# Weights issued at the turn, two more pairs transposed on TensorE, and one scores chunk moved up in a fused attention and MLP kernel

## The chip, the cores and the metric

One core of a Trainium2 chip. The metric is device time in microseconds of a whole execution. The kernel before has a median of 423.64 us (3 runs, 423.2 to 425.69). A trace's span is 1.7 to 1.8 us shorter than the time of the same run.

## The reference

```
scores = q k^T / 8 ; attn = softmax(scores) ; x = attn v      # 8 batches, 12 heads, 448 tokens, 64 wide
h = x[3584,768] @ w_in[768,2048] ; out = leaky_relu(h, 0.01) @ w_out[2048,768]
```

## The kernel before

Two heads of one batch are a "pair"; there are 48. Pairs 0 to 5 run alone (`first`); then each batch's MLP runs on TensorE with the attention of later pairs cut in between it as "clusters". All loads up to pair 17 (but k and v of pair 0) and all weights go through GpSimd's queue, which casts float32 to bfloat16 on the way; SP issues the later loads, the DMA transposes and the stores. q and k have to be transposed before the scores matmul: on TensorE (into PSUM, with a copy back by VectorE) below `NPE`, by a DMA transpose from `NPE` on; `NXP` does the same for x. A pair's scores come in four "chunks" of 112 keys, and w_out is loaded in four "pieces".

```
    NXP = 9
    NPE = 12
    def dma_transposes(u):
        if NPE <= u < NU:
            turn(qkT[u % NQ][:, :QL], qk_sb[u].rearrange("p i so h d -> p (i so h d)"))
    # ... transposes(u): eight nc.tensor.transpose and one nc.vector.tensor_copy, for u < NPE

    def first(u):
        # ... scores and expo of chunks 0 and 1
        if u >= 1:
            pv(u - 1, 0)
        transposes(u + 1)
        # ... casts and loads
        if u > 0:
            scores(u, 2)
        scores(u, 3)

    def cluster(g):
        # ... transposes(turn_q) if turn_q < NPE, scores, expo, pv, x_transposes
        if r < 3:
            cast(u + 3 + r)
            load(u + 5 + r)
            load_w({9: 1, 10: 1, 13: 1}.get(g, 0))
        if r > 0:
            dma_transposes(u + 2 + r)

    # the turn between the pairs of `first` and the clusters
    transposes(HP + 1)
    cast(HP + 3)
```

The first batch's second matmul takes output columns 0 to 383 for all its rows first, then columns 384 to 767. The last w_out piece (rows 1024 to 2047 of those last columns) is therefore wanted latest.

The softmax here doesn't subtract the row's maximum and nothing guards it: scores larger than these inputs give would overflow.

Of the kernel before, what the change touches and what calls it, by code (L numbers as in the profile page):

```python
# [16 lines left out]
def kernel(  # L17
# [101 lines left out]
    def load(u):  # L119
        if u >= NU:  # L120
            return
        if u < NSW:
            if u % 2 == 0:
                load_soft(u, 2, (0, 1, 2))
            return
        for x in range(3):
            load_one(u, x, nc.sync)

    def cast(u, parts=(0, 1, 2), by=nc.gpsimd.tensor_copy):
        if u >= NU:  # L130
            return
        for x in parts:
            f = raw[u].pop(x)
            if u not in qk_sb:
                qk_sb[u] = cast_pool.tile([SC, 2, NSC, 2, D], BF16, name="qkb")
            if x < 2:
                by(qk_sb[u][:, x].rearrange("p so h d -> p h so d"), f)  # L137
            else:
                by(v_sb[u % NV][:, :, :, :D], f)  # L139
# [8 lines left out]
    def load_w(n=1):  # L148
        for _ in range(n):
            if w_steps:  # L150
                o, i = w_steps.pop(0)
                nc.gpsimd.dma_start(out=o, in_=i)
# [21 lines left out]
    def warm_up(n):  # L174
        for _ in range(n):
            ps = ps_g.tile([P, 512], F32, name="mm", tag="g")
            nc.tensor.matmul(ps, warm[:, :P], warm, start=True, stop=True)
# [15 lines left out]
    x_t = {}  # L193

    NXP = 9
    NPE = 12

    def turn(dst, src):
        nc.sync.dma_start_transpose(out=dst.rearrange("p (c s) -> p c s", s=SC), in_=src)
# [4 lines that stand above are left out]
# [6 lines left out]
    def turn_tile(bank):  # L210
        if bank is None:
            return ps_g.tile([P, 2, S], BF16, name="tr", tag="g")
        return bank.bitcast(BF16)[:, :2 * S].rearrange("p (i s) -> p i s", i=2)

    def transposes(u, bank=None):
        if u >= min(NPE, NU):
            return
        for parts in ((1,), (0,)) if u == 0 else ((0, 1),):
            tr = turn_tile(bank)
            for i in parts:  # L220
                for so in range(NSC):
                    nc.tensor.transpose(  # L222
                        tr[:, i, ts(so, SC)], qk_sb[u][:, i, so], ident[:SC, :SC]
                    )
            at = slice(parts[0], parts[-1] + 1)
            nc.vector.tensor_copy(  # L226
                qkT[u % NQ][:, :QL].rearrange("p (i s) -> p i s", i=2)[:, at], tr[:, at]
            )
# [3 lines left out]
    def scores(u, c):  # L232
        ps = ps_s.tile([P, 2, 512], F32, name="sc", tag="sc")
        t = qkT[u % NQ]
        sc_t[u, c] = ps
        for j in range(2):
            nc.tensor.matmul(  # L237
                ps[:, j, :S],
                t[j * D:(j + 1) * D, S + c * SC:S + c * SC + P],
                t[j * D:(j + 1) * D, :S],  # L240
                start=True, stop=True,
            )

    def expo(u, c):
        e = e_sb[u % NE][:, :EL].rearrange("p (j c s) -> p j c s", j=2, c=NSC)
        nc.scalar.activation(e[:, :, c, :], sc_t.pop((u, c))[:SC, :, :S], AX.Exp, scale=scale)  # L246

    def pv(u, j, bank=None):

        e, vt = e_sb[u % NE], v_sb[u % NV]  # L250
        if bank is None:
            ps = ps_g.tile([P, NSC, D + 1], F32, name="pv", tag="g")
        else:
            ps = bank[:, :NSC * (D + 1)].rearrange("p (q d) -> p q d", q=NSC)
        for qc in range(NSC):
            for c in range(NSC):
                at = (j * NSC + c) * S + qc * SC
                nc.tensor.matmul(  # L258
                    ps[:, qc, :], e[:, at:at + P], vt[:, j, c, :],
                    start=(c == 0), stop=(c == NSC - 1),  # L260
                )
        if j == 0:
            x_t[u] = x_pool.tile([SC, NSC, 2, D], BF16, name="x")
        rec = r_pool.tile([SC, NSC, 1], F32, name="rec")
        nc.vector.reciprocal(rec, ps[:SC, :, D:])  # L265
        nc.vector.tensor_mul(  # L266
            x_t[u][:, :, j, :], ps[:SC, :, :D], rec.to_broadcast([SC, NSC, D])
        )

    def x_transposes(u, bank=None):  # L270
        b, hp = divmod(u, HP)
        at = b * S % NX
        dst = xT[:, hp, at:at + S]
        if u >= NXP:
            turn(dst, x_t.pop(u).rearrange("p so h d -> p (so h d)"))
            return
        tr = turn_tile(bank)
        for so in range(NSC):
            nc.tensor.transpose(tr[:, 0, ts(so, SC)], x_t[u][:, so], ident[:SC, :SC])  # L279
        nc.vector.tensor_copy(dst, tr[:, 0, :])  # L280
# [72 lines left out]
    def supply(u):  # L353

        for what, n in {0: [('qk', 2), ('v', 1), ('v', 2), ('load', 6)], 1: [('qk', 3), ('qk', 4), ('v', 3), ('w', 1)], 2: [('qk', 5), ('v', 4), ('v', 5), ('load', 8)], 3: [('qk', 6), ('v', 6), ('w', 1)], 4: [('qk', 7), ('v', 7), ('w', 1)], 5: [('qk', 8), ('v', 8), ('load', 10), ('w', 1)]}[u]:
            if what == "qk":
                cast(n, (0, 1), fast if n in (2, 3) else nc.gpsimd.tensor_copy)
            elif what == "v":
                cast(n, (2,))
            elif what == "load":  # L360
                load(n)
            else:
                load_w(n)

    def first(u):

        scores(u, 0)
        scores(u, 1)
        expo(u, 0)
        if u == 0:  # L370
            warm_up(2)
        expo(u, 1)
        if u == 0:
            scores(u, 2)
        if u >= 2:
            x_transposes(u - 2)
        if u >= 1:
            pv(u - 1, 0)
        transposes(u + 1)
        if u + 1 < HP:  # L380
            supply(u)
        if u > 0:
            scores(u, 2)
        scores(u, 3)
        expo(u, 2)
        expo(u, 3)
        if u + 1 == HP:
            supply(u)
        if u >= 1:
            pv(u - 1, 1)  # L390


    def cluster(g):
        t, r = divmod(g, 4)
        u = 3 * t
        chunks = [divmod(4 * u + 3 * r + x, NSC) for x in range(3)]
        chunks = [(a, c) for a, c in chunks if a < NU]
        heads = [[(u - 1, 0)], [(u - 1, 1)], [(u, 0), (u, 1)], [(u + 1, 0), (u + 1, 1)]][r]
        heads = [(a, j) for a, j in heads if HP <= a < NU]
        turn_q = {3: u + 3, 0: u + 1, 1: u + 2}.get(r, NU)  # L400
        turn_x = {0: u - 2, 2: u - 1, 3: u}.get(r, 0)
        if turn_q < NPE:
            transposes(turn_q)
        elif len(heads) > 1:
            pv(*heads.pop(0))
        for a, c in chunks:
            scores(a, c)
        for a, c in chunks[:2]:
            expo(a, c)
        late.extend(chunks[2:])  # L410
        if HP <= turn_x < NXP:
            x_transposes(turn_x)
        for a, j in heads:
            pv(a, j)
            if j == 1 and a >= NXP:
                x_transposes(a)
        if r < 3:
            cast(u + 3 + r)
            load(u + 5 + r)
            load_w({9: 1, 10: 1, 13: 1}.get(g, 0))  # L420
        if r > 0:
            dma_transposes(u + 2 + r)

# [2 lines left out]
    for u in range(HP):  # L426
        first(u)
# [14 lines left out]
    expo(HP, 2)  # L442
    x_transposes(HP - 1)
    transposes(HP + 1)
    cast(HP + 3)


# [4 lines left out]
    for i in range(B):  # L452
        work = list(range(begin[i], begin[i + 1])) if i + 1 < B else []
        n = cuts[i + 1] - cuts[i]
        total = MD * KD * n + n // P * MD * DM
        used, done, groups = 0, 0, 0

        def catch_up():
            nonlocal done
            while done < len(work) and (  # L460
                groups >= early[done] if i == 0 else used * len(work) >= total * (done + 1)
            ):
                settle()
                cluster(work[done])
                done += 1

        catch_up()
        for step in mlp(i):
            used += step
            groups += 1  # L470
            catch_up()
# [30 lines left out]
```

## Time and profile before

| what | where | value |
|---|---|---|
| median time | runs | 423.64 us |
| span of the traced run (it took 424.84) | page | 423.1 us |
| TensorE busy | page | 408.6 us, 97% |
| longest wait of TensorE | its waits | 4.6 us, once, for a piece of w_out |
| granted clock after that wait | windows | 0.50 for 5 us |

The prediction shows the lines and reads them.

### The profile page before, as it was taken

To read this page: it belongs to the slowest core of one execution; us is meant where nothing else is said; L and a number is where in the kernel's file an instruction comes from. 1 tells how busy PE (TensorE), PEld (TensorE's weight loads), DVE (VectorE), ACT (ScalarE), POOL (GpSimd) and SP (SyncE) were. 2 spreads that over 40 slices of the span, in tenths; PEclk is the share of its full clock that TensorE was granted. 3 is DMA by queue.
4 is the path that set the end of the run, shared out by engine and by line. 5 is a ranking of instruction groups with operands and counts; after the bars stand their busy time and mean duration, and the time that the engine had idled before them with its cause. 6 is when DMAs were issued, how large, how long until landed. Compare 5 with 4: busy or idle time off the path is not lost.

```text
span 423.1 us, 8937 instructions
## 1 busy us (share of the span) xinstructions
PE 408.6 (97%) x3726; PEld 235.1 (56%) x3726; DVE 103.2 (24%) x292; ACT 228.9 (54%) x324; POOL 105.0 (25%) x177
## 2 busy tenths in 40 slices
PE   7999996999999999999999999999999999999995
PEld 3566663454556656554565656654465666654563
DVE  3652431120132212221132212321032311320021
ACT  5888872266724684467634486456752577214300
POOL 7775744320311211131131213131120200000000
PEclk9899999799999999999999999999999999999999
DMA  8999999884475957779465785769275420230022
GB/s 130 192 201 203 173 174 155 159 222 99 107 159 156 209 109 183 188 138 196 98 156 143 198 147 134 193 134 239 57 170 147 118 56 14 60 85 2 0 76 75
DMA packets 98121, 57.69 MB, mean 136 GB/s; under 512 B 55072, under 2 KB 94496, under 8 KB 98080
## 3 DMA queue, kind: packets, MB, share of 16 engines
q1 hardware_dynamic: 78448, 44.63, 46.7%
q0 software_dynamic: 19392, 12.26, 20.8%
q8 instruction: 29, 0.48, 0.5%
q10 hardware_dynamic: 240, 0.23, 0.2%
q14 instruction: 12, 0.10, 0.1%
HBM read 45.61 MB, written 11.01 MB: 134 GB/s over the span
## 4 chain that ended last, share of the span: by engine, by line
PE 87%; DMA 8%; POOL 2%; DVE 1%; issue 1%; POOLq 0%
PE mm L343 33%; PE mm L314 32%; PE pv L258 12%; PE sc L237 9%; DMA w_out_sb<-in_moe_w_out_dram 4%; DMA fv<-in_v_dram 2%; DMA fk<-in_k_dram 2%; PE tr L222 1%; POOL fq L102 1%; PE tr L279 1%; PE sc L314 1%; DVE x L266 1%; POOL fk L102 0%; POOL v L139 0%; DVE o L347 0%
## 5 line engine op out<-in xcount | busy, mean ns | idle before, releaser
L246 ACT ACTIVATE e<-sc 112x896 bf16<-112x896 f32 x192 | 164.8, 915 | 107.3 <-PE sc L237 107.0
L343 PE MATMUL mm<-w_out_sb,h 128*128 128x384 bf16 x896 | 151.7, 328 | 4.8 <-DMA w_out_sb<-in_moe_w_out_dram 4.6
L314 PE MATMUL mm<-xT,w_in_sb 128*128 128x512 bf16 (+1 forms) x756 | 148.6, 353 | 0.2 <-DVE x L266 0.2
L343 PEld LDWEIGHTS <-h 128*128 128x128 bf16 x896 | 86.3, 98 | 60.6 <-issue 6.3
L314 PEld LDWEIGHTS <-w_in_sb 128*128 128x128 bf16 x768 | 72.9, 98 | 66.2 <-issue 1.2
L329 ACT ACTIVATE h<-mm 128x512 bf16<-128x512 f32 (+1 forms) x126 | 68.7, 545 | 58.7 <-PE mm L314 58.6
L258 PEld LDWEIGHTS <-e 112*128 112x128 bf16 x1536 | 57.3, 98 | 26.7 <-issue 16.2
L139 POOL CAST v<-fv 112x512 bf16<-112x512 f32 x30 | 18.5, 616 | 196.6 <-PE pv L258 184.7
L258 PE MATMUL pv<-v,e 112*128 112x65 bf16 x1536 | 66.1, 195 | 0.2 <-ACT e L246 0.2
L347 DVE COPY o<-mm 128x384 f32<-128x384 f32 x56 | 31.2, 558 | 139.5 <-PE mm L343 139.5
L265 DVE RECIPROCAL rec<-pv 112x4 f32<-112x4 f32 x96 | 17.5, 182 | 152.5 <-PE pv L258 151.8
L237 PE MATMUL sc<-qkT 64*128 64x448 bf16 x384 | 50.2, 361 | 0.9 <-DVE qkT L226 0.9
L266 DVE TENSOR_TENSOR x<-pv,rec 112x256 bf16<-112x256 f32 x96 | 40.7, 424 | 3.5 <-DVE rec L265 0.2
L237 PEld LDWEIGHTS <-qkT 64*128 64x128 bf16 x384 | 13.8, 95 | 18.9 <-issue 10.5
L137 POOL CAST qkb<-fk 112x512 bf16<-112x512 f32 x30 | 18.4, 613 | 0.1
L137 POOL CAST qkb<-fq 112x512 bf16<-112x512 f32 x30 | 18.4, 613 | 0.1
L139 POOL COPY v<-fv 112x512 bf16<-112x512 bf16 x17 | 10.4, 620 | 17.6 <-DMA fv<-in_v_dram 9.0
L137 POOL COPY qkb<-fq 112x512 bf16<-112x512 bf16 x14 | 8.7, 620 | 13.1 <-DMA fq<-in_q_dram 13.1
L226 DVE COPY qkT<-tr 128x896 bf16<-128x896 bf16 (+1 forms) x13 | 7.6, 585 | 8.6 <-PE tr L222 8.5
L137 POOL COPY qkb<-fk 112x512 bf16<-112x512 bf16 x14 | 8.7, 618 | 2.7 <-DMA fk<-in_k_dram 2.7
L222 PE MATMUL tr<-ident,qkb 112*128 112x112 bf16 x96 | 7.6, 219 | 1.3 <-DVE qkb L137 1.3
L222 PEld LDWEIGHTS <-qkb 112*128 112x128 bf16 x96 | 6.0, 100 | 3.3 <-DVE qkb L137 1.8
(30 smaller groups left out, 51.9 us busy)
## 6 DMA issues: line engine op xcount, KB each, us to landing
fk<-in_k_dram SPq DMA_DIRECT2D x31, 224.0 KB, 3.4
fq<-in_q_dram SPq DMA_DIRECT2D x30, 224.0 KB, 3.3
fv<-in_v_dram SPq DMA_DIRECT2D x30, 224.0 KB, 3.8
w_in_sb<-in_moe_w_in_dram POOLq DMA_DIRECT2D x4, 768.0 KB, 11.4
w_out_sb<-in_moe_w_out_dram POOLq DMA_DIRECT2D x4, 768.0 KB, 13.5
out_dram<-o SPq DMA_DIRECT2D x8, 336.0 KB, 2.9
out_dram<-o SPq DMA_DIRECT2D x8, 288.0 KB, 2.6
out_dram<-o SPq DMA_DIRECT2D x8, 240.0 KB, 3.4
```

Source lines behind the costliest of these rows:

```text
L137: by(qk_sb[u][:, x].rearrange("p so h d -> p h so d"), f)
L139: by(v_sb[u % NV][:, :, :, :D], f)
L222: nc.tensor.transpose(tr[:, i, ts(so, SC)], qk_sb[u][:, i, so], ident[:SC, :SC])
L237: nc.tensor.matmul(ps[:, j, :S], t[j * D:(j + 1) * D, S + c * SC:S + c * SC + P], t[j * D:(j + 1) * D, :S], start=True, stop=True,)
L246: nc.scalar.activation(e[:, :, c, :], sc_t.pop((u, c))[:SC, :, :S], AX.Exp, scale=scale)
L258: nc.tensor.matmul(ps[:, qc, :], e[:, at:at + P], vt[:, j, c, :], start=(c == 0), stop=(c == NSC - 1),)
L265: nc.vector.reciprocal(rec, ps[:SC, :, D:])
L266: nc.vector.tensor_mul(x_t[u][:, :, j, :], ps[:SC, :, :D], rec.to_broadcast([SC, NSC, D]))
L314: nc.tensor.matmul(open_t[m][:, :n], w_in_sb[:, kk, ts(m, P)], xT[:, kk, at:at + n], start=(fresh and kk == kks[0]), stop=(kk == KD - 1),)
L329: nc.scalar.activation(h[:, m, :n], open_t.pop(m)[:, :n], AX.Prelu, alpha=0.01)
L343: nc.tensor.matmul(ps[:, :NW], h[:, m, ts(c, P)], w_out_sb[:, m, ts(w, NW)], start=(m == 0), stop=(m == MD - 1),)
L347: nc.vector.tensor_copy(o[c][:, ts(w, NW)], ps[:, :NW])
```

## The change

The intent: have the last weights there in time, take two transposes off the DMA engines while those are loaded with weights and inputs, and give ScalarE its next scores before TensorE stops for the casts of pair 2. The title it came with also names a new spacing of one-transfer pairs and q of the first pair on SP; its diff, complete here, has neither.

```
-    NPE = 12
+    NPE = 14
@@ first(u)
         if u >= 1:
             pv(u - 1, 0)
+        if 0 < u < 2:
+            scores(u, 2)
         transposes(u + 1)
         if u + 1 < HP:
             supply(u)
-        if u > 0:
+        if u >= 2:
             scores(u, 2)
@@ cluster(g)
-            load_w({9: 1, 10: 1, 13: 1}.get(g, 0))
+            load_w({9: 1, 10: 1}.get(g, 0))
@@ the turn
     transposes(HP + 1)
+    load_w()
     cast(HP + 3)
```

More of the change, by code (lines that the diff above doesn't have):

```diff
@@ L195 @@
     NXP = 9
-    NPE = 12
+    NPE = 14
     def turn(dst, src):
@@ L378, in first @@
             pv(u - 1, 0)
+        if 0 < u < 2:
+            scores(u, 2)
         transposes(u + 1)
@@ L381, in first @@
             supply(u)
-        if u > 0:
+        if u >= 2:
             scores(u, 2)
@@ L419, in cluster @@
             load(u + 5 + r)
-            load_w({9: 1, 10: 1, 13: 1}.get(g, 0))
+            load_w({9: 1, 10: 1}.get(g, 0))
         if r > 0:
@@ L444 @@
     transposes(HP + 1)
+    load_w()
     cast(HP + 3)
```

## The prediction

> **What bounds the kernel now.** I read the page's busy shares first, then what TensorE waited for, then the chain that ended last in order of time, then windows around the one hole it shows, then the timelines of the engines that issue the transfers concerned.
>
> ```profile
> PE 408.6 (97%) x3726; PEld 235.1 (56%) x3726; DVE 103.2 (24%) x292; ACT 228.9 (54%) x324; POOL 105.0 (25%) x177
> ...
> PEclk9899999799999999999999999999999999999999
> ```
>
> TensorE is busy 408.6 of 423.1 us; no other engine is over 56%. So work put on TensorE costs its full length, and a gain can come only from TensorE's 14.5 us of idle time or from its clock. The clock row has two dips: slice 2 and slice 8 (a slice is 10.6 us, so slice 8 is 74 to 85 us).
>
> ```profile
> PE mm L343 <- DMA w_out_sb<-in_moe_w_out_dram: 4.6, 1, 4.6
> PE tr L222 <- DVE qkb L137: 1.3, 2, 0.7
> ```
>
> The waits of TensorE hold one large entry: a single 4.6 us for a piece of w_out. The second, 1.3 us in two waits, is for the cast of q and k ahead of TensorE transposes. About 4.6 us before the first data-fed work and 4.2 us of final store (418.8 to 423) are the rest; the change touches neither.
>
> ```profile
> 57.45 17.51 DMA w_out_sb<-in_moe_w_out_dram
> 75.00 2.72 PE mm L343 x8
> 77.72 1.24 PE sc L237 x6
> 78.95 0.99 PE pv L258 x16
> 79.94 5.29 PE mm L343 x32
> 85.74 0.67 PE sc L237 x6
> 86.42 0.62 PE pv L258 x16
> ```
>
> This is the chain. The last w_out piece is issued at 57.45 and lands at 75.0. The work after it is slow: six scores matmuls take 1.24 where the next six take 0.67, sixteen PV matmuls 0.99 against 0.62. The windows say why:
>
> ```profile
> 66.00:70.40 4.40, 4.40 (x40) 2.71 (x38) 1.16 (x3) 2.17 (x3) 0.61 (x1) 1.00 1.59 143
> 70.40:75.00 4.60, 0.03 (x2) 0.00 (x0) 0.00 (x0) 0.00 (x0) 4.13 (x7) 0.80 1.31 139
> 75.00:76.50 1.50, 1.50 (x5) 0.71 (x5) 0.00 (x0) 0.00 (x0) 0.24 (x1) 0.50 1.45 197
> ```
>
> Columns: stretch, then busy time of PE, PEld, DVE, ACT, POOL, granted clock, DMA share, GB/s. TensorE is idle from 70.4 to 75, and comes back at clock 0.50; the windows keep it near 0.5 until 80 and show 1.00 after. From 80 us to the last matmul TensorE has no wait worth a row.
>
> **What the Trainium skill says.** (1) "TensorE: Matmul & The Clock Gate", section "What's actually happening": after about one idle window (some 3.4 us) the array runs at half clock, and some 3.4 us of sustained work free it. The trace agrees: 4.57 us idle, then 0.50 for about 5 us. (2) "DMA: Bandwidth & Descriptors", section "Issuing engines are not separate DMA queues": transfers of SP, ACT and GpSimd share the same 16 DMA engines. The trace agrees: a transpose of q and k on SP, median 4.0 us to landing, took 11.2 and 12.3 when issued at 50.39 and 58.15 among the loads. (3) Same page, "Two DMAs through the same engine are not ordered": descriptors start in order within a queue. Landings on GpSimd's queue around 45 to 75 do come in order of issue (below). (4) "TensorE: Matmul & The Clock Gate", "Part 4: PE-mode transpose": it needs a VectorE copy out of PSUM afterwards; the trace has that copy, 0.62 us.
>
> **The change part by part.** The title also names spacing of the software queue and q of the first pair on SP; the diff holds no such edit, so I price only the diff.
>
> *Weights earlier.* GpSimd issues in program order:
>
> ```profile
> 34.71 0.90 POOL L152 DMA_DIRECT2D w_out_sb<-in_moe_w_out_dram  x1
> 45.77 0.90 POOL L152 DMA_DIRECT2D w_out_sb<-in_moe_w_out_dram  x1
> 48.32 0.88 POOL L152 DMA_DIRECT2D w_out_sb<-in_moe_w_out_dram  x1
> 57.45 0.89 POOL L152 DMA_DIRECT2D w_out_sb<-in_moe_w_out_dram  x1
> ```
>
> The new call sits in the turn between the first pairs and the clusters, just ahead of the cast of pair 9, which ran at 35.6. So the second piece goes out at about 35.6 instead of 45.8, the third at 45.8 instead of 48.3, the fourth at about 49 instead of 57.45: each takes its predecessor's place.
>
> When do they land? Issue plus time to landing, from the DMA view window by window: first piece 46.9; q, k, v of pairs 12/13 48.1, 49.7, 52.7; second piece 57.0; third 63.1; q, k, v of 14/15 65.0, 66.8, 70.8; fourth 75.0. That is one saturated queue. A load of 2 pairs reads 0.46 MB (2 pairs x 2 heads x 448 x 64 x 4 B), a piece 1.57 MB (768 x 2048 x 4 B / 4), so 7.46 MB land in 28.1 us, 265 GB/s. At that rate (estimate) the three loads of a group take 5.2 us. The new order is piece 1, piece 2, 12/13, piece 3, piece 4, 14/15. The total is the same, so the last piece is done at 75.0 - 5.2 = 69.8 at the latest; two transposes leave the DMA engines (next part), which should bring it to 66 to 69. TensorE wants it at 70.4 or, with the added transposes, 71.5. So I expect the wait gone: **-4.57 us**.
>
> With the hole goes the clock dip. Excess over the same work at full clock: matmuls 2.72 - 8 x 5.20/32 = 1.42, scores 1.24 - 0.67 = 0.57, PV 0.99 - 0.62 = 0.37, the next 32 matmuls 5.29 - 5.20 = 0.09. Sum **-2.45 us**.
>
> *TensorE transposes for pairs 12 and 13.* Removes two DMA transposes on SP (50.39 and 58.15); adds 16 transposes and two VectorE copies of 0.62. In the chain eight transposes occupy TensorE 0.53, so **+1.06 us** on the bound engine. The copies lie beside: VectorE is 24% busy, and the scores of pair 12 come one cluster later. PSUM rotation is a bit tighter (two PV back to back after a transpose); the cluster at 41.6 us has this pattern already and costs 0.18. I add **+0.2**.
>
> *Scores of chunk 2 ahead of the transposes, pair 1.*
>
> ```profile
> 11.82 0.55 PE L222 MATMUL tr<-ident,qkb 112*128 112x112 bf16 x4 [0.71 <-DVE qkb L137]
> ...
> 12.90 3.59 ACT L246 ACTIVATE e<-sc 112x896 bf16<-112x896 f32 x4 [1.01 <-PE sc L237]
> ```
>
> (First line from TensorE's timeline, second from ScalarE's.) TensorE is in order: it waits 0.71 for k of pair 2, and the scores behind it starve ScalarE for 1.01. Issued before the transposes they fill that hole. ScalarE then works nearly without a break until 28.3, so it paces this stage; up to 1.0 us could come forward, less what TensorE at half clock (12 to 15 us) and the loads hold back. I take **-0.7 us**.
>
> *Sum:* -4.57 - 2.45 + 1.06 + 0.2 - 0.7 = -6.46; 423.64 - 6.46 = **417.2 us**, a gain of 1.5%.
>
> **Rivals.**
>
> (A) *A new wait takes the old one's place: pair 14.* Its loads now stand behind two pieces and are issued after the delayed pair 12 casts, near 57.5 instead of 53.35. Its k should land near 70 to 71.5 (before: 66.8), the cast takes 0.6, then SP transposes; that took 8.1 us to landing in the crowd at 67.49, 4.0 as the median. So 75.5 to 80. Pair 14 is first read as the third chunk of the cluster that ran at 85.67: new time about 80 (85.67 - 7.02 + 1.06, plus two scores at 0.45). A near thing: against it, 0 to 4 us of slack; for it, a queue less emptied than I think. It would give back 1 to 3 us, and over 3.4 us the clock dip too: 419 to 422. One in seven.
>
> (B) *Pair 12 late for TensorE.* Its load now lands behind the second piece: q and k near 54 to 56 instead of 48.1 and 49.7. TensorE's transposes of it start at about 58. Slack some 1 to 2 us; a miss costs about 1 us.
>
> (C) *The piece is still late.* 69.8 without any relief against a need at 71.5, and issue is early enough, so at most a fraction of a us.
>
> (D) *The weights' wait was hidden anyway.* No: TensorE's 0.03 us busy in 4.60, and a chain that runs through that transfer, speak against it.
>
> (E) *More than I count:* relief from the DMA transposes and the early start could also save the first clock dip (about 1.5 us at 12 to 15). That gives 416.
>
> **Range and chances.** The clock and the wait together are 7.0 us and should go as one; the additions are firm. Best plausible 423.64 - 7.0 - 1.5 - 0.5 + 1.2 = about 415.8; A or B in part gives about 420.2. For over 2% the time has to fall under 415.2, which needs every item at its best: 5%. Slower by over 2% means over 432, a new stall far beyond the one removed: 2%.
>
> **What would show it.** Right: no w_out row in TensorE's waits over 0.5 us; clock near 1.00 from 70 to 80; 112 transposes for q and k on TensorE (now 96) and 34 on SP (now 36); the last w_out issue near 49 and landed before 70; ScalarE's idle before its second run of exponentials near 0 instead of 1.01; the end of the span earlier by the same 6 to 7 us that the start of the 96-matmul run (376.71 in the chain) is. Wrong: a row of TensorE waiting for the transposed q and k of pair 14 near 78 to 82, or for the cast of pair 12 near 58, with a clock dip behind it; or an idle GpSimd queue, which would mean that the saturation I count on isn't there.

## The result, and the profile after

418.73 us (median of 4 runs, 418.22 to 419.01) against 424.25 (4 runs) in the same rounds: ratio 0.9866, interval 0.9832 to 0.99. A ratio here is the mean time of one kernel's runs over that of the other's of the same rounds, so it is not quite the ratio of the medians. Two later sets of rounds with the same pair gave 0.9903 and 0.9897. So the change is faster, by 1.0 to 1.3%, which is within 2%; the time is inside the range of 415.8 to 420.2 and 1.5 us over the point of 417.2.

The page after, busy shares and clock:

```profile
PE 407.5 (98%) x3742; PEld 235.2 (56%) x3742; DVE 103.5 (25%) x294; ACT 228.9 (55%) x324; POOL 105.1 (25%) x177
...
PEclk9999999999999999999999999999999999999999
```

TensorE has 16 instructions more, VectorE two more, as priced; both dips of the clock row are gone. What TensorE waited for, the whole list (line, releaser, us in total, times, longest):

```profile
PE mm L177 <- DVE gate L170: 1.2, 1, 1.2
PE tr L279 <- DVE x L266: 1.0, 3, 0.5
PE sc L237 <- DVE qkT L226: 0.7, 2, 0.5
PE tr L222 <- DVE qkb L137: 0.3, 1, 0.3
PE mm L343 <- DVE x L266: 0.2, 1, 0.2
PE mm L314 <- DVE x L266: 0.2, 1, 0.2
```

No DMA is in it. The same stretches as in the prediction's windows, in the same columns:

```profile
70.40:75.00 4.60, 4.60 (x44) 2.59 (x42) 1.16 (x3) 2.36 (x3) 2.36 (x5) 1.00 1.14 171
75.00:76.50 1.50, 1.50 (x12) 0.91 (x10) 0.32 (x1) 0.17 (x1) 1.07 (x2) 1.00 0.59 166
```

TensorE is busy through the old hole, at clock 1.00. GpSimd's weight issues in the timeline, where the first two pieces are now one line of two:

```profile
34.38 1.77 POOL L152 DMA_DIRECT2D w_out_sb<-in_moe_w_out_dram  x2
46.00 0.90 POOL L152 DMA_DIRECT2D w_out_sb<-in_moe_w_out_dram  x1
48.55 0.89 POOL L152 DMA_DIRECT2D w_out_sb<-in_moe_w_out_dram  x1
```

The last piece goes out at 48.55 and by the DMA view needs 14.5 us, so it lands at 63.1 (before: 75.0). The transposes added on TensorE in that stage, and the run of w_out matmuls that used to stop after 24 of its 32:

```profile
65.20 0.56 PE L222 MATMUL tr<-ident,qkb 112*128 112x112 bf16 x8
65.69 0.74 PE L237 MATMUL sc<-qkT 64*128 64x448 bf16 x6
66.36 0.68 PE L258 MATMUL pv<-v,e 112*128 112x65 bf16 x16
66.88 5.36 PE L343 MATMUL mm<-w_out_sb,h 128*128 128x384 bf16 x32
```

From here to the end the two traces hold the same work in nearly the same time: the span is 6.3 us shorter and the second batch's MLP, which starts at 80.38 instead of 86.87, already has 6.5 of it.

### The profile page after: what moved, and what is told of

It reads as the page before. It is cut to its first block, busy times and chain, and to the rows that moved or that the text cites. A ratio compares the mean times of both kernels' runs of the same rounds, so it can differ in the third digit from the quotient of the medians.

```text
span 416.8 us, 8966 instructions
## 1 busy us (share of the span) xinstructions
PE 407.5 (98%) x3742; PEld 235.2 (56%) x3742; DVE 103.5 (25%) x294; ACT 228.9 (55%) x324; POOL 105.1 (25%) x177
## 4 chain that ended last, share of the span: by engine, by line
PE 95%; DVE 2%; DMA 1%; issue 0%; POOLq 0%
PE mm L343 35%; PE mm L314 35%; PE pv L258 13%; PE sc L237 10%; PE tr L222 2%; DMA fq<-in_q_dram 1%; DVE x L266 1%; PE tr L279 1%; PE sc L314 1%; DVE o L347 0%; DVE qkT L226 0%; DVE rec L265 0%; PE mm L177 0%; DVE qkb L137 0%; DVE xT L280 0%
## 5 line engine op out<-in xcount | busy, mean ns | idle before, releaser
L258 PE MATMUL pv<-v,e 112*128 112x65 bf16 x1536 | 65.2, 194 | 0.0
L265 DVE RECIPROCAL rec<-pv 112x4 f32<-112x4 f32 x96 | 17.5, 182 | 150.1 <-PE pv L258 149.6
L226 DVE COPY qkT<-tr 128x896 bf16<-128x896 bf16 (+1 forms) x15 | 8.8, 588 | 11.2 <-PE tr L222 11.2
L222 PE MATMUL tr<-ident,qkb 112*128 112x112 bf16 x112 | 8.8, 225 | 0.3 <-DVE qkb L137 0.3
L222 PEld LDWEIGHTS <-qkb 112*128 112x128 bf16 x112 | 7.2, 103 | 2.7 <-ACT qkb L188 0.6
```

Of the source, the lines that this page charges most:

```text
L222: nc.tensor.transpose(tr[:, i, ts(so, SC)], qk_sb[u][:, i, so], ident[:SC, :SC])
L258: nc.tensor.matmul(ps[:, qc, :], e[:, at:at + P], vt[:, j, c, :], start=(c == 0), stop=(c == NSC - 1),)
L265: nc.vector.reciprocal(rec, ps[:SC, :, D:])
```

## The experiments

Two theories to start with. **A:** the wait went because the last piece is issued 8.9 us earlier; the TensorE transposes only cost. **B:** it went because two DMA transposes left the DMA engines, so the queue catches up whenever the piece is issued.

| kernel | median us (runs) | ratio to before, 95% |
|---|---|---|
| weights earlier alone | 417.77 (6) | 0.9870, 0.9832 to 0.9908 |
| TensorE transposes alone | 418.65 (6) | 0.9901, 0.9861 to 0.9941 |
| scores order alone | 423.88 (6) | 1.0008, 0.9963 to 1.0053 |
| weights and scores order | 417.31 (6) | 0.9862, 0.9820 to 0.9903 |
| the changed kernel, second set | 419.49 (6) | 0.9903, 0.9868 to 0.9938 |
| TensorE transposes, and dummy DMA transposes | 423.30 (6) | 0.9991, 0.9964 to 1.0018 |
| before, hole filled with matmuls | 422.38 (6) | 0.9968, 0.9942 to 0.9994 |
| changed, TensorE transposes through pair 17 | 422.04 (6) | 0.9960, 0.9932 to 0.9989 |
| the changed kernel, third set | 418.65 (6) | 0.9897, 0.9861 to 0.9933 |
| weights and scores order, third set | 417.25 (4) | 0.9855, 0.9817 to 0.9893 |
| changed, TensorE transposes through pair 12 | 418.71 (5) | 0.9891, 0.9856 to 0.9926 |
| before, unedited, for a second trace | 423.17 (4) | 0.9995, 0.9955 to 1.0036 |

The first four share rounds with one set of runs of before (median 423.60), the next four with another (423.21), the next three with a third (423.81), the last with a fourth (423.62). Kernels are compared only within the same rounds.

**1. The weights alone.**

```
-            load_w({9: 1, 10: 1, 13: 1}.get(g, 0))
+            load_w({9: 1, 10: 1}.get(g, 0))
...
+    load_w()
     cast(HP + 3)
```

> Weights earlier alone (TensorE transposes still to pair 11, scores order as before). Theory A (the earlier issue removes the w_out wait and the clock dip, the two added TensorE transposes only cost): w_out wait 0, time 424.2 - 7.0 = about 417.2, that is 0.5 us under the changed kernel (it lacks +1.25 of transposes and also -0.7 of the scores order). Theory B (it is the two DMA transposes leaving the DMA engines that let the queue catch up): the last piece lands after 69, or pair 13's transposed q and k (landed 70.4 before) become a new wait of 1 to 4 us near 72; time 419 to 423.

417.77, and no w_out wait and no wait for transposed q and k in TensorE's list. Theory A's number. The last piece, issued at 49.17, took 15.7 us (the last number of its line in the DMA view) and landed at 64.9, with both DMA transposes still in the crowd, that is among the loads and weights of 45 to 75 us:

```profile
w_out_sb<-in_moe_w_out_dram POOLq DMA_DIRECT2D x1, 768.0 KB, 15.7
```

That is 10.1 us earlier than in the first trace of before, 9.3 than in the second, where the prediction had 5.2 for the order alone.

**2. The transposes alone.**

```
-    NPE = 12
+    NPE = 14
```

> TensorE transposes through pair 13 alone. Theory A: the last piece still goes out near 57.5 behind the loads of pairs 14/15, lands after 72, wait of 1 to 4 us and the clock dip stay in part; time 423 to 425. Theory B: the queue is freed of two transposes, the piece lands before 71.4, no wait; 424.2 - 7.0 + 1.25 = about 418.5.

418.65: theory B's number too. The last piece is issued late as before, at 55.93 (before: 57.45 and, in the second trace, 55.65), but takes 13.4 us instead of 17.5 (18.6 in the second trace) and lands at 69.3:

```profile
w_out_sb<-in_moe_w_out_dram POOLq DMA_DIRECT2D x1, 768.0 KB, 13.4
```

TensorE's timeline of this kernel, the run that used to break:

```profile
66.91 5.36 PE L343 MATMUL mm<-w_out_sb,h 128*128 128x384 bf16 x32
```

The 32 matmuls go through without a stop. The piece is wanted after 24 of them, at 66.91 + 24 x 0.1625 = 70.8 (0.1625 is 5.20 / 32), so it was 1.5 us early. Experiments 1 and 2 together: either edit is enough alone. Their gains do not add, because they remove one and the same wait; the changed kernel, which has both, gains no more within the noise (ratios 0.9866, 0.9903 and 0.9897 in its three sets) than the weights alone (0.9870).

**3. The scores order alone.**

```
+        if 0 < u < 2:
+            scores(u, 2)
         transposes(u + 1)
...
-        if u > 0:
+        if u >= 2:
```

> Scores of chunk 2 of pair 1 ahead of the transposes alone. My theory: ScalarE's 1.0 us idle near 12 goes, TensorE's first MLP group starts 0.7 us earlier, but everything then waits for the last w_out piece, which the queue lands at 75 whatever TensorE does: time within 0.5 us of before. Rival: the start sets the end, 423.5 (-0.7).

No difference. The wait is still in TensorE's list:

```profile
PE mm L343 <- DMA w_out_sb<-in_moe_w_out_dram: 3.6, 1, 3.6
```

While the piece's arrival sets the time, being earlier at it buys nothing.

**4. Weights and scores order, without the transposes** (edits 1 and 3 together).

> The whole change without the TensorE transposes of pairs 12 and 13. Theory A: 418.7 - 1.25 = about 417.4, faster than the changed kernel. Theory B: a wait for pair 12's or 13's transposed q and k or for the last piece gives back 1 to 4 us: 418.5 to 421.

417.31, the fastest so far, by 0.46 under experiment 1 in the same rounds; the runs of the two overlap (416.8 to 418.1 against 417.1 to 418.2), so what the scores order gains is suggested, not settled. The 1 us of theory B is there in this trace, from a transfer the prediction did not name: the transposed x of the second batch.

```profile
PE mm L314 <- DMA xT<-x: 1.0, 1, 1.0
```

It did not come again when the kernel was repeated (below).

**5. The changed kernel again.** No edit.

> The changed kernel again, unedited, so that it shares its rounds with the next three: about 418.7.

419.49, and its runs split: three at 418.3 to 418.8, three at 420.2 to 421.3. Its trace is of a run of 420.2, with a span of 418.4 against 416.8. The timelines show where the 1.6 us are: one and the same run of w_in matmuls, first in the changed kernel's trace, then in this one:

```profile
43.77 2.11 PE L314 MATMUL mm<-xT,w_in_sb 128*128 128x384 bf16 x12 [0.18 <-DVE x L266]
```

```profile
45.43 2.11 PE L314 MATMUL mm<-xT,w_in_sb 128*128 128x384 bf16 x12 [0.18 <-DVE x L266]
```

So all of it comes from the start, where the granted clock of this trace is 0.50 from 8 to 14 us (1.00 in the first trace from 10 to 14) and TensorE waits 1.5 us, until 6.18, for the cast of q of pair 0, which itself waited 1.4 us for its load. The start differs from run to run by as much as the small terms of the prediction.

**6. TensorE transposes, but the DMA transposes too.** The kernel of experiment 2, with SP still turning pairs 12 and 13, into tiles that nobody reads.

```
     def dma_transposes(u):
+        if u in (12, 13):
+            turn(spare[u - 12], qk_sb[u].rearrange("p i so h d -> p (i so h d)"))
```

> TensorE transposes through pair 13 alone (418.65 before), but SP still issues the two DMA transposes of pairs 12 and 13, into tiles nobody reads. Theory (two DMA transposes in the crowd cost GpSimd's queue 5 to 6 us: the last piece landed near 69 without them and at 75 with them): the w_out wait comes back with 2.5 to 4.5 us and with it the clock dip; 423.5 to 426. Rival (their work on TensorE or their order is what helped): no w_out wait, 418.7.

423.30, as slow as before; time and wait both lie just under the ranges expected. The wait is back, though TensorE needs neither result. TensorE's waits, then the windows (columns as before):

```profile
PE mm L347 <- DMA w_out_sb<-in_moe_w_out_dram: 2.3, 1, 2.3
```

```profile
71.00:73.40 2.40, 0.07 (x1) 0.00 (x0) 0.00 (x0) 0.00 (x0) 0.04 (x1) 0.95 1.44 90
73.40:74.50 1.10, 1.08 (x4) 0.56 (x4) 0.00 (x0) 0.00 (x0) 0.00 (x0) 0.50 2.13 106
```

```profile
w_out_sb<-in_moe_w_out_dram POOLq DMA_DIRECT2D x1, 768.0 KB, 18.0
```

The piece, issued at 55.36, took 18.0 us and landed at 73.4. Against 13.4 us in experiment 2, the two transposes cost it 4.6 (one trace each). That is theory B's mechanism, shown with nothing else changed.

**7. The hole filled.** The kernel before, with matmuls nobody reads ahead of the one that waits.

```
                 for m in range(MD):
+                    if i == 0 and c == 0 and w == 1 and m == MD // 2:
+                        fill = ps_g.tile([P, 512], F32, name="mm", tag="g")
+                        for _ in range(20):
+                            nc.tensor.matmul(fill, warm[:, :P], warm, start=True, stop=True)
```

> The kernel before with 20 idle-filling 128x512 matmuls (some 4.3 us) ahead of the matmul that waits for the last piece. The wait stays: the transfer is untouched. Theory (idle[...] halves the clock and costs 2.45 us on top): clock 1.00 from 75 to 80, time 2.0 to 2.5 us under before. Rival (the wait alone is the cost): time as before.

TensorE's timeline:

```profile
70.14 4.48 PE L346 MATMUL mm<-warm 128*128 128x512 bf16 x20
74.45 1.46 PE L347 MATMUL mm<-w_out_sb,h 128*128 128x384 bf16 x8
```

The piece landed at 74.4, as the fill ended. The first eight matmuls after it take 1.46 where they took 2.72, and the clock reads 1.00 from 70 to 80 us. So the dip is a cost of its own and follows from idleness. By the runs it is worth 0.8 us (medians) to 1.4 us (ratio 0.9968), less than the 2.0 to 2.5 expected. A likely reason, not shown: the fill has a fixed length, and in runs with a shorter wait it overruns it (experiment 12 has a wait of 3.6).

**8. More pairs on TensorE.** The changed kernel with `NPE = 18`.

> The changed kernel with TensorE transposes through pair 17 instead of 13: 32 more transposes, 4 x 0.53 to 0.6 us on the bound engine, nothing waiting on DMA transposes to win: 418.7 + 2.1 to 2.6 = about 421. Rival (the relief of the DMA engines pays for them): 418.7 or less.

422.04 against 419.49 in the same rounds: 2.55 us for four pairs by the medians, 0.64 per pair (by the means 2.31 and 0.58). With the wait gone, moving these transposes to TensorE was only a cost.

**9, 10, 11. The changed kernel, the version without its transposes, and `NPE = 13`,** in the same rounds.

> The changed kernel unedited, to share rounds with the next two: 418.7 to 419.5.

> The change without its TensorE transposes, in the same rounds as the changed kernel. Theory (the earlier weights alone remove the wait; each pair transposed on TensorE costs 0.64, as four more pairs cost 2.55): 1.3 under the changed kernel, less up to 1.0 for the wait for the transposed x that its first profile shows: 0.3 to 1.3 faster. Rival (relief of the DMA engines pays for the two transposes): equal within 0.3.

> The changed kernel with TensorE transposes through pair 12 only. Theory: half of the cost back, 0.6 under the changed kernel, and one DMA transpose fewer in the crowd than above, so no wait for transposed x: between the two, or the best of the three. Rival: equal to the changed kernel.

418.65, 417.25 and 418.71. The version of experiment 4 beats the changed kernel by 1.4 us, and its four runs lie between 417.17 and 417.36. Its list of waits holds no DMA this time. The middle version was expected 0.6 under the changed kernel and is not; its traced run (419.81) has no wait over 0.2 us that the other lacks. In that trace the w_in run shown under experiment 5 starts at 45.63, against 43.83 in the other, so its start was slow; where the median's 0.6 went stays open.

**12. A second trace of before.** No edit.

> The kernel before, unedited, for a second trace of it. Theory (the first trace shows a long wait: its run took 424.84, the median is 423.6 and runs go from 419.1 to 426.2, so the wait for the last w_out piece and the clock dip behind it are shorter in most runs): where the run is under 424, wait plus dip together under 7.0 us, 4 to 6.5. Rival (they are the same in each run and the spread comes from the start of the kernel): 4.6 us of wait again and half clock for about 5 us.

The traced run took 423.41, near the median. Its wait in TensorE's list, and the matmuls behind it in the timeline:

```profile
PE mm L343 <- DMA w_out_sb<-in_moe_w_out_dram: 3.6, 1, 3.6
```

```profile
74.26 2.53 PE L343 MATMUL mm<-w_out_sb,h 128*128 128x384 bf16 x8 [3.61 <-DMA w_out_sb<-in_moe_w_out_dram]
76.73 1.30 PE L237 MATMUL sc<-qkT 64*128 64x448 bf16 x6
77.96 0.69 PE L258 MATMUL pv<-v,e 112*128 112x65 bf16 x16
```

At full clock these take 1.46, 0.74 and 0.68 in the same view, so the dip costs 1.07 + 0.56 + 0.01 = 1.64, and wait and dip together 5.25. In the first trace the same sum, with the wait of 4.57, is 6.9. So the theory holds: the wait varies with the run. No trace caught a run of before under 421 us; what those few lack stays open.

## Why the prediction was right, and where it was off

**What bounds the kernel: right.** TensorE's single wait for w_out and the clock dip behind it were the time to be won, and both went. The fill of experiment 7 shows the dip as a cost apart from the wait.

**"-4.57" and "-2.45", together -7.0: right mechanism, wrong size.** They came from one trace of a run that took 424.84, 1.2 us over the median. A trace of a run near the median gives 3.61 + 1.64 = 5.25. The weights alone, which do nothing else, gained 1.3% of 423.60, which is 5.5. This term carries nearly all of the error: 7.0 - 5.25 = 1.8, against a point that was 1.5 too low.

**"+1.06" and "+0.2" for the transposes: right.** 1.26 for two pairs was predicted. The changed kernel minus the version without them is 1.40, and experiment 8 gives 2 x 0.64 = 1.28; experiment 2 less experiment 1, a third estimate, is 0.88.

**"-0.7" for the scores order: not shown.** In the changed kernel's first trace ScalarE's idle of 1.01 is gone; 0.43 is left before a run of exponentials that goes through:

```profile
10.30 17.37 ACT L246 ACTIVATE e<-sc 112x896 bf16<-112x896 f32 x21 [0.43 <-PE sc L237]
```

With the wait away, 0.46 us is measured (experiment 4 less 1) with overlapping runs, and the start varies by more: from the first to the end of the 24th exponential it takes 20.6 to 21.4 us in the six traces with the old order and 20.4 to 22.3 in the eight with the new one.

The sum with the sizes measured is -5.25 + 1.3 - 0.5 = -4.5; the three sets give -1.34%, -0.97% and -1.03%, or -5.7, -4.1 and -4.4 us.

**"One saturated queue" at 265 GB/s: wrong as a rate.** It put the last piece at 66 to 69 and k of pairs 14/15 at 70 to 71.5. They landed at 63.1 and 65.4. Counted as in the prediction, the same bytes (7.47 MB; its 7.46 is rounding) landed between 47.1 and 67.2 (v of 14/15: issue 56.56 and 10.6 us), 372 GB/s. So the queue was not at a rate of its own. The same count takes 28.1 us before (27.6 in its second trace), 22.9 in experiment 1, 22.9 in experiment 2, 20.1 with both edits and 27.4 in experiment 6. The DMA transposes held it up: the prediction named that relief but made it 1 to 4 us where experiment 6 measures 4.6. And the order alone shortened it as much: in two windows of 2 us from 48 on, where the DMA view shows no packet of a transpose yet, 134 and 160 GB/s move before (169 and 182 in its second trace) and 140 and 175 in experiment 2, but 199 and 197 in experiment 1, where one piece more is already queued. Why less moves without that piece is not shown. The prediction thus made both reliefs too small; it was luck that this does not show in the time, as any landing before about 71 us does. It did not see that the transposes alone would have been enough, and that one edit makes the other a cost.

**Rivals.** A (pair 14 late) did not happen: its DMA transpose went out at 66.06 and took 2.9 us, not the feared 4 to 8; the queue's last load of that group had landed at 67.2 instead of 70 or later. B (pair 12 late) did not: its k was cast at 53.34, transposed at 57.40. C and D are ruled out by TensorE's waits and by the gain. E (the start also saving its dip) depends on the run: the first trace of the changed kernel has no dip from 12 to 15, the second has.

## What to carry to other kernels

When a late transfer stalls the bound engine, ask both what shares the DMA engines with it and when it is issued: here two transposes of 0.23 MB each held it up for 4.6 us, and an earlier issue alone brought it 9 to 10 us forward. Two edits that remove the same wait don't add, so try each alone; the one with a cost (transposes on the bound engine) was not needed, and leaving it out beat the changed kernel by 1.4 us and the kernel before by 6. Take the size of a wait from more than one trace when runs differ by more than the effect.

## What the Trainium skill lacked or had wrong

- "TensorE: Matmul & The Clock Gate", "What's actually happening", gives about 3.4 us of idle window before the clock halves. In experiment 6 TensorE came back at 0.50 after an idle gap of 2.34 us (before it, the clock was 1.00), so a shorter gap can do it. By windows of 0.2 to 0.5 us the clock fell some 2.1 us after TensorE stopped there, 2.7 in the first trace of before and 3.8 in the second, there just after it had started again (estimates from the means of those windows).
- "Advanced Engine Details and Errata", "X-Bar Transpose (TRN2)", says that transpose DMAs are as fast as regular ones. Over the whole kernel that fits roughly (before: 4.0 us median to landing, against 3.3 to 3.8 for a load of 224 KB on the same queue). In the crowd it doesn't: two transposes of 0.23 MB each put off a plain load by 4.6 us. At the rate at which the changed kernel's queue wrote (3.73 MB in 20.1 us) their 0.46 MB would be 2.5 us, an estimate from those numbers. No page gives what a transpose takes from loads beside it.
